# A fused attention and expert-routing kernel: an earlier third sum in phase 0, phase 1 in a fixed list, expert 1 in halves of rows

## The chip, the core and the metric

The kernel runs on one core of a Trainium2 chip. A core has TensorE (PE in the rows, with PEld for its weight loads), VectorE (DVE), ScalarE (ACT), GpSimd (POOL) and SyncE (SP, which here only issues DMAs). Each engine takes its instructions in the order of its own list and waits on semaphores for the others. The metric is the device time of one execution in microseconds, lower is better.

## The reference

Attention over a band of 128 positions gives x (4608 tokens by 512). Then a greedy routing: all 4608 x 8 pairs of token and expert are walked in falling order of their logit; a token goes to the expert of the first pair at which it is still free and the expert has under 576 tokens. Each expert is a two-layer network with a ReLU.

```python
logits = x @ w_gate
order = np.argsort(-logits.flatten())
for idx in order:
    tok, e = (int(idx) // E, int(idx) % E)
    if assigned[tok] >= 0 or counts[e] >= cap:
        continue
    assigned[tok] = e
    counts[e] += 1
...
for e in range(E):
    mask = assigned == e
    h = np.maximum(x[mask] @ w1[e], 0.0)
    out[mask] = h @ w2[e]
```

## The kernel before

Attention takes the first 185 us or so; the change leaves it as it is. Behind it the work is a chain of eight *phases* of routing and eight experts. A phase finds which expert fills up next and at which logit: it counts on PE, by products of 0/1 matrices with ones, how many tokens lie above each of 64 thresholds, narrows the interval, and does that three times (`few`, with the 16 best candidates of each partition). Then it sums the members (`totals`), numbers them (`members`, `positions`, `hits`) and writes the row numbers of the 576 tokens of that expert to `idx` (`rows`). `later` masks the logits for the next phase; two additions of it run on POOL from phase 1 on. Phase 0 (`phase0`) is written apart: it does part of its sums during attention, and guesses the first expert after one search step, so that the first two tiles of rows ("early tiles") and the expert's weights are asked for before the search ends.

An expert takes five tiles of rows. POOL gathers each tile from DRAM into `g`; PE transposes it into a PSUM tile (`pg`, one buffer, or `po`); ACT casts it to `xh`, and DVE takes the rest `xl` from the same PSUM tile (`flip` and `under`; `turn` does both, tile by tile). Weights come in four chunks a layer through `raw` (four buffers) and are split as well: ACT casts the high part (`high`), DVE makes the low part in two halves (`low`; rows `hl<-raw,hl`). Each product is then three matmuls (high by high, high by low, low by high). Layer 1 runs over f = 0 to 7; in `layer1` both column groups of rows (0 to 287, 288 to 575) go through in turn for each f. Layer 2 runs over the five tiles and POOL scatters each finished tile. `keep_warm(n)` puts n matmuls of zeros on PE.

What sets the order: instructions given through `OrderedCore` stand on PE, DVE and ACT in the order in which the program writes them; through `OrderedTensor` only PE's do; given through plain `nc` a scheduler places them by its own estimates. In `first_expert` all is in written order, and generators are stepped by hand: `go` steps phase 0, `next(route)` steps phases 1 to 7, which run one behind the other in the generator `route`. A step issues everything up to the next `yield`. After `first_expert` the kernel before goes over to `OrderedTensor`: in expert 0's layer 2, 40 steps, the tables at L426 to L429 say at which step a piece of `route` is written (`ROUTE_2`), a chunk asked for (`LOAD_2`), split (`SPLIT_2`), the gather issued (`GATHER_2`) and a tile transposed (`TURN_2`). From expert 1 on `slot` does this by due times (`W_LOAD`, `W_SPLIT`) and by the waits that `route` yields.

## Time and profile before

| what | value |
|---|---|
| three runs | 707.56 to 711.46 us, median 709.33 |
| profiled execution | 710.49 us |
| its span (first to last instruction) | 708.6 us |
| PE busy, share of the span | 94% |
| DVE, ACT, POOL busy | 65%, 46%, 21% |

The share of busy time is a mean over stages, and a matmul at the lower clock is counted as busy like one at the higher. So the rows below read stages and single waits. A row of a timeline begins with the start in us and the time in us, then engine, line, operation, output and inputs by the names above; x4 at its end means four instructions merged, and the square bracket holds how long the engine stood idle before it and for whom. Most lines of this stretch carry L461, the line of the helper that keeps the written order, so the names tell them apart. A row of a table by stage has the stretch and its length, then busy us and (instructions) of PE, PEld, DVE, ACT and POOL, the mean granted clock of PE as a share of 2.4 GHz, and the DMA engines' busy share and GB/s.

### The profile page before, as it was taken

How to read it: one execution, taken by the hardware profiler on the slowest of the kernel's cores; microseconds unless marked ns; L12 is line 12 of the kernel's file. 1: busy time of each engine (PE TensorE's matmuls, PEld its weight loads, DVE VectorE, ACT ScalarE, POOL GpSimd, SP SyncE). 2: the span in 40 equal slices, each digit the busy share in tenths (PEclk: the TensorE clock that was granted, in tenths of full speed). 3: DMA queues.
4: the chain of work that ended last, by engine and by line, in shares of the span. 5: the costliest groups of instructions: out<-in, count | busy, mean ns of one | idle time of the engine just before them, and what ended most of it. 6: DMA issues, size and time to landing. Idle time of an engine off the chain costs nothing.

```text
span 708.6 us, 18904 instructions
## 1 busy us (share of the span) xinstructions
PE 667.4 (94%) x7272; PEld 584.4 (82%) x7273; DVE 460.2 (65%) x1903; ACT 326.3 (46%) x992; POOL 150.3 (21%) x337
## 2 busy tenths in 40 slices
PE   8999999999947998599899999999999999999996
PEld 5899889988845976388679879988988988988986
DVE  6778888888876877575778859756864724523210
ACT  6998898988832521422423324314324324323211
POOL 4122222222201102301411324032033023011011
PEclk9999999999975999699999999999999999999999
DMA  8475757575324403700913617145134434401001
GB/s 292 161 229 175 225 178 224 176 229 177 116 78 137 145 8 103 255 9 7 313 46 127 200 57 244 58 134 175 64 119 130 125 98 136 140 21 40 8 24 48
DMA packets 35139, 92.72 MB, mean 131 GB/s; under 512 B 3808, under 2 KB 13152, under 8 KB 35040
## 3 DMA queue, kind: packets, MB, share of 16 engines
q1 hardware_dynamic: 29152, 72.55, 31.7%
q0 software_dynamic: 5888, 18.88, 8.0%
q8 instruction: 59, 0.97, 0.6%
q14 instruction: 40, 0.33, 0.1%
HBM read 72.54 MB, written 18.87 MB: 129 GB/s over the span
## 4 chain that ended last, share of the span: by engine, by line
PE 79%; DVE 9%; issue 4%; DMA 4%; ACT 3%; SPq 0%; POOL 0%; POOLq 0%; DVEq 0%; ACTq 0%
PE ph L1105 22%; PE po L1147 8%; PE po L1148 8%; PE pt L53 6%; PE x L53 6%; PE po L1150 6%; PE s L53 6%; PE pt L160 6%; PE ph L461 4%; PE po L461 2%; DMA g<-x,idx 2%; ACT u L147 2%; PE pg L1077 2%; DVE hl L1042 1%; DMA raw<-in_w_dram 1%
## 5 line engine op out<-in xcount | busy, mean ns | idle before, releaser
L1105 PE MATMUL ph<-xh,hl 128*128 128x288 f32 x896 | 164.3, 298 | 0.0
L1105 PEld LDWEIGHTS ph<-xh,hl 128*128 128x128 f32 x896 | 134.0, 189 | 0.9
L147 ACT ACTIVATE u<-u,mn 128x192 f32<-128x192 f32 (+2 forms) x288 | 124.1, 440 | 5.8 <-DVE mn L137 5.8
L1147 PE MATMUL po<-hl,hh 128*128 128x512 f32 (+1 forms) x288 | 115.2, 400 | 0.5 <-ACT hh L1111 0.5
L1148 PE MATMUL po<-hl,hh 128*128 128x512 f32 (+1 forms) x288 | 111.4, 387 | 0.0
L1111 ACT ACTIVATE hh<-ph 128x288 fp32r<-128x288 f32 x112 | 40.4, 409 | 132.3 <-PE ph L1105 132.2
L1105 PE MATMUL ph<-xl,hl 128*128 128x288 f32 x448 | 97.8, 297 | 0.0
L137 DVE CUSTOM_DVE_ANT_0 u<-s,bm 128x192 f32<-128x192 f32 (+1 forms) x248 | 71.8, 345 | 30.5 <-PE s L53 29.9
L1150 PE MATMUL po<-hl,hlo 128*128 128x512 f32 (+1 forms) x232 | 89.3, 385 | 0.0
L1159 POOL DMA_INDIRECT out_dram<-o,idx x38 | 41.3, 1086 | 204.4 <-ACT o L1154 131.5
L1042 DVE TENSOR_TENSOR hl<-raw,hl 128x512 fp32r<-128x512 f32 x112 | 73.6, 683 | 13.5 <-ACT hl L1036 13.0
L1105 PEld LDWEIGHTS ph<-xl,hl 128*128 128x128 f32 x448 | 72.4, 189 | 0.0
L1084 DVE TENSOR_TENSOR xl<-pg,xh 128x512 fp32r<-128x512 f32 (+1 forms) x35 | 22.3, 636 | 74.3 <-ACT xh L1078 74.0
L1122 DVE SCALAR_TENSOR_TENSOR hlo<-ph,hh 128x288 fp32r<-128x288 f32 x112 | 43.1, 416 | 39.6 <-ACT hh L1111 39.2
L1036 ACT CAST hl<-raw 128x1024 fp32r<-128x1024 f32 x56 | 57.4, 1049 | 20.4 <-DMA raw<-in_w_dram 16.1
L1154 ACT COPY o<-po 128x512 f32<-128x512 f32 (+1 forms) x33 | 18.9, 574 | 103.2 <-PE po L1150 51.6
L1147 PEld LDWEIGHTS po<-hl,hh 128*128 128x128 f32 x288 | 54.5, 189 | 10.5 <-ACT hh L1111 0.7
L1148 PEld LDWEIGHTS po<-hl,hh 128*128 128x128 f32 x288 | 54.6, 189 | 9.4
L53 PE MATMUL s<-qk 64*64 64x192 f32 (+1 forms) x992 | 60.0, 326 | 0.6 <-DVE mn L137 0.5
L147 ACT ACTIVATION_READ_ACCUMULATOR u<-u,mn 128x1 f32 x288 | 56.4, 196 | 0.0
L1058 POOL DMA_INDIRECT g<-x,idx x38 | 40.4, 1062 | 72.1 <-PE pg L1077 22.9
L160 PE MATMUL pt<-ident_sb,u 128*128 128x128 f32 x368 | 52.8, 279 | 0.7 <-ACT u L147 0.4
(308 smaller groups left out, 1120.0 us busy)
## 6 DMA issues: line engine op xcount, KB each, us to landing
raw<-in_w_dram SPq DMA_DIRECT2D x64, 512.0 KB, 4.2
qk<-in_qk_dram SPq DMA_DIRECT2D x32, 576.0 KB, 5.1
v<-in_v_dram SPq DMA_DIRECT2D x32, 288.0 KB, 4.0
x<-xb SPq DMA_DIRECT2D x14, 512.0 KB, 3.6
x<-xb SPq DMA_DIRECT2D x8, 128.0 KB, 3.4
x<-xb SPq DMA_DIRECT2D x4, 256.0 KB, 2.3
g<-x,idx POOLq DMA_INDIRECT x38, 5.1
out_dram<-o,idx POOLq DMA_INDIRECT x38, 2.9
```

The source lines that it names most:

```text
L53: put(nc.tensor.matmul(out, w, a, start=start, stop=stop, skip_group_check=True))
L137: put(nc.vector.tensor_tensor_reduce(out=weights(n, t, h), in0=x[:, c:c + 64 * m].rearrange("q (j k) -> q j k", k=64), in1=bm[n % NP][:, y ...
L147: put(nc.scalar.activation(u, u, AF.Exp, bias=st["mn"][:, i:i + 1], scale=-1.0, accum_out=st["sm"][:, i:i + 1]))
L160: put(nc.tensor.transpose(ps[:, c:c + 128], u[:, o + 128 * j:o + 128 * j + 128], ident))
L461: return lambda *a, **k: self.tc.keep_in_program_order(getattr(self.engine, name)(*a, **k))
L1036: self.nc.scalar.copy(hl[:, 0, :], raw)
L1042: self.nc.vector.tensor_tensor(hl[:, 1, c:c + 512], raw[:, c:c + 512], hl[:, 0, c:c + 512].bitcast(F32), ALU.subtract)
L1105: self.nc.tensor.matmul(pp[t], w[:, a, j, fo:fo + 128], x[:, j, cut[t]:cut[t + 1]], start=(j == 0 and a == 0 and x is xh), stop=(j == 3 an ...
L1122: self.nc.vector.scalar_tensor_tensor(d, pp[t][:, c0:c1], 0.0, o[:, c0:c1].bitcast(F32), ALU.max, ALU.subtract)
L1147: nc.tensor.matmul(out, a, wh, start=(f == 0), stop=False)
L1148: nc.tensor.matmul(out, a, wl, start=False, stop=(f == 7 and t == 4))
L1150: nc.tensor.matmul(out, hl[:, f, 128 * t:128 * t + 128], wh, start=False, stop=(f == 7))
```

## The change

Four things change. In phase 0 `yield` is added behind the sum of each search step, and the calls in `first_expert` are regrouped so that the last step's sum is written ahead of the second early tile's transposes; the zero matmuls are shared out anew, and one operation (`hi`) goes behind `members`. Expert 0's second weights are asked for one piece earlier, and all their low halves are written ahead of phase 1's third piece. `OrderedTensor` goes: expert 0's layer 2 stays in written order on PE, DVE and ACT; only the pieces of `route` behind phase 1's row numbers, and the gathers, are left to the scheduler. Phase 1 is stepped at 26 steps at the latest instead of 29, the gather follows at once, and two pieces of phase 2 (`ROUTE_3`) and the weights of expert 1 come behind. In expert 1 phase 2 is stepped in every slot (`SOONER`), and its layer 1 runs over the first half of the rows for all f, then over the second.

```diff
-ZEROS = 1, 4, 1, 3, 4
...
-ROUTE_2 = 11, 13, 15, 17, 19, 21, 22, 25, 29
...
+ZEROS = 2, 4, 1, 2, 5
...
+ROUTE_2 = 11, 12, 14, 15, 17, 18, 19, 22, 26
+ROUTE_3, SOONER = (33, 37), (1, 2)
...
@@ -804,6 +806,7 @@
                 next(n)
             except StopIteration as e:
                 n = e.value
+            yield
             if s == 1:
                 lo2 = self.small("lo")
                 nc.vector.scalar_tensor_tensor(lo2, w, n[:, 0:1], low, ALU.mult, ALU.add)
@@ -812,8 +815,8 @@
         sel, rest = (rt.tile([128, NT], BF, name=name, bufs=1) for name in ("sel0", "rsel"))
         nc.vector.tensor_scalar(sel, key[:, :, 0], 1.0, n[:, 0:1], ALU.add, ALU.is_ge)
         nc.vector.tensor_tensor(rest, self.rest, sel, ALU.mult)
+        m, ex = self.members(am, v[:, 0:1], rest, NT)
         nc.vector.scalar_tensor_tensor(self.hi, w, n[:, 0:1], low, ALU.mult, ALU.add)
-        m, ex = self.members(am, v[:, 0:1], rest, NT)
         sp = self.bank()
         self.positions(sp, m, ex, NT)
         nc.tensor.matmul(sp[:, 64:65], self.C["ones"], self.run[:, NT - 1:NT], start=True, stop=True)
@@ -894,6 +897,8 @@
         self.rows(ip, hits, NT, 5, idx)
         self.idx[k] = [idx[:, t:t + 1] for t in range(5)]
         self.later(k, L, T1, Dc, keyv, mx)
+        if k == 1:
+            yield 0
 
     def later(self, k, L, T1, Dc, keyv, mx):
 
@@ -1121,14 +1126,17 @@
                     c0, c1 = c0 - cut[t], c1 - cut[t]
                     self.nc.vector.scalar_tensor_tensor(d, pp[t][:, c0:c1], 0.0, o[:, c0:c1].bitcast(F32), ALU.max, ALU.subtract)
 
-    def layer1(self, w1):
+    def layer1(self, w1, halves=False):
 
         self.hidden()
         cut = 0, 288, 576
-        for f in range(8):
-            yield from self.steps1(w1, f, cut, (0, 1))
-            self.rest1(self.pp, f, cut, (0, 1))
+        for f, ts in [(f, (t,)) for t in range(2) for f in range(8)] if halves else [(f, (0, 1)) for f in range(8)]:
+            for _ in self.steps1(w1, f, cut, ts):
+                if not halves:
+                    yield
+            self.rest1(self.pp, f, cut, ts)
             yield
+
 
     def layer2(self, w2, h, idx, last=False, fine=False):
         nc = self.nc
@@ -1207,11 +1215,6 @@
         o += w
 
 
-class OrderedTensor:
-    def __init__(self, tc):
-        self.vector, self.scalar, self.sync, self.tensor = tc.nc.vector, tc.nc.scalar, tc.nc.sync, Ordered(tc, tc.nc.tensor)
-
-
 def first_expert(tc, P, C, r, m, route):
 
     nc = tc.nc
@@ -1250,16 +1253,16 @@
     m.idle = P["ps_h"].tile([128, 512], F32, name="ph")
     W = [m.high(raw[c]) for c in range(2)]
     go(2)
+    m.low(W[0], raw[0], 0)
     m.keep_warm(ZEROS[0])
-    m.low(W[0], raw[0], 0)
-    go()
+    go(2)
+    m.low(W[0], raw[0], 1)
     m.keep_warm(ZEROS[1])
-    m.low(W[0], raw[0], 1)
     go(2)
     m.low(W[1], raw[1], 0)
     a0 = m.flip(*ga[0], "o")
     m.keep_warm(ZEROS[2])
-    go()
+    go(2)
     a1 = m.flip(*ga[1])
     m.keep_warm(ZEROS[3])
     go()
@@ -1295,14 +1298,14 @@
     rest(4, 0)
     b = m.flip(*gb[0], "o")
     m.under(*b)
+    late = marked(1)
+    second += ask(late, 1, range(1, 4))
     layer(6, 0)
     rest(5, 0)
     b = [m.flip(*gb[1], "o"), m.flip(*gb[2])]
     m.under(*b[0])
     rest(6, 0)
     m.under(*b[1])
-    late = marked(1)
-    second += ask(late, 1, range(1, 4))
     layer(7, 0)
     rest(7, 0)
     V, lows = [], []
@@ -1310,16 +1313,17 @@
         layer(f, 1)
         if f == 0:
             go()
-        if f % 2 == 0:
-            V.append(m.high(second[f // 2]))
-            lows += [(V[-1], second[f // 2], half) for half in range(2)]
+        if f in HIGHS_2:
+            V.append(m.high(second[len(V)]))
+            lows += [(V[-1], second[len(V) - 1], half) for half in range(2)]
         if f:
             rest(f - 1, 1)
-        for _ in range(CHOICE_1.get(f, 0)):
+        if f in CHOICE_1:
             next(route)
-        for _ in range(LOWS_2.get(f, 0)):
+        for _ in range(LOWS_2[f]):
             m.low(*lows.pop(0))
     rest(7, 1)
+    next(route)
     return V
 
 
@@ -1344,6 +1348,8 @@
         st["wait"] -= 1
         if st["wait"] <= 0 and (k + 1 not in r.idx or k + 2 not in r.idx and i >= AHEAD[min(k, 2)]):
             st["wait"] = next(route, 0)
+            if k == 1 and k + 1 not in r.idx:
+                st["wait"] = SOONER[i == 0]
         for e, layer, c, due in W_LOAD:
             e += k
             if i >= due and e in r.ei and len(raws.get((e, layer), ())) == c:
@@ -1373,28 +1379,30 @@
             next(route)
     else:
         V = first_expert(tc, P, C, r, m, route)
-        r.nc = m.nc = OrderedTensor(tc)
     i = 0
     for _ in m.layer2(V, m.h, r.idx[0], fine=True):
         i += 1
         if i in ROUTE_2 and not exact:
             next(route)
-        if i == GATHER_2:
+        if i == ROUTE_2[-1]:
+            r.nc = nc
             gathers[0] = m.turn(m.gather(r.idx[1]))
+        if i in ROUTE_3:
+            next(route)
         for _ in range(LOAD_2.get(i, 0)):
             load(1, 0)
         if i in SPLIT_2:
             part(1, 0)
         if i in TURN_2:
             next(gathers[0])
+    r.nc = m.nc = nc
     while len(W[1, 0]) < 4:
         part(1, 0)
     for _ in gathers[0]:
         pass
-    r.nc = m.nc = nc
     for k in range(1, E):
         i = 0
-        for _ in m.layer1(W.pop((k, 0))):
+        for _ in m.layer1(W.pop((k, 0)), k == 1):
             slot(k, i)
             i += 1
         for _ in range(9):
```

The order on PE behind the counts of phase 0's last search step (sat is their verdict, whose sum with the ones is meant; po and pg are the two early tiles, zero the zero matmuls, ex the input of the positions). Before:

```order
L461 MATMUL po<-ident_sb,g 128x128 x4
L461 LDWEIGHTS zero
L461 MATMUL ph<-zero 128x512
L461 MATMUL pg<-ident_sb,g 128x128 x4
L461 LDWEIGHTS zero
L461 MATMUL ph<-zero 128x512
L461 LDWEIGHTS zero
L461 MATMUL ph<-zero 128x512
L461 LDWEIGHTS zero
L461 MATMUL ph<-zero 128x512
L461 LDWEIGHTS c_ones
L461 MATMUL m<-sat,c_ones 128x1
```

and now:

```order
L463 MATMUL po<-ident_sb,g 128x128 x4
L463 LDWEIGHTS zero
L463 MATMUL ph<-zero 128x512
L463 LDWEIGHTS c_ones
L463 MATMUL m<-sat,c_ones 128x1
L463 MATMUL pg<-ident_sb,g 128x128 x4
L463 LDWEIGHTS zero
L463 MATMUL ph<-zero 128x512
L463 LDWEIGHTS zero
L463 MATMUL ph<-zero 128x512
L463 LDWEIGHTS c_ones
L463 MATMUL m<-ex,c_ones 128x36
```

The sum of sat has moved ahead of the second tile and of three zero matmuls; two of the zeros now stand between the tile and ex.

The order on DVE at the end of phase 1 (loOH and mv are the inputs of the row numbers, io to idx their end; am and OH belong to phase 2's first piece, as do the b, ne, cand and ext that stand further up before; hl are weight halves of expert 1, xl its tiles). Before:

```order
L736 TENSOR_TENSOR loOH<-c_i_429,slo 128x2304
L728 TENSOR_TENSOR mv<-hOH,c_cc 128x36x10
L730 TENSOR_SCALAR mv<-hOH,craw 128x36x10
L515 TENSOR_TENSOR OH<-c_eb,am 128x288
L1042 TENSOR_TENSOR hl<-raw,hl 128x512
L749 COPY io<-m 64x20
L1042 TENSOR_TENSOR hl<-raw,hl 128x512
L751 TENSOR_TENSOR ia<-m,io 64x20
L1042 TENSOR_TENSOR hl<-raw,hl 128x512
L754 SCALAR_TENSOR_TENSOR idx<-ia 64x5 x2
L1042 TENSOR_TENSOR hl<-raw,hl 128x512 x5
L1084 TENSOR_TENSOR xl<-pg,xh 128x4x128
```

and now, from the masks that follow idx:

```order
L463 TENSOR_TENSOR flag<-flag,ov 128x1
L463 TENSOR_TENSOR hl<-raw,hl 128x512 x2
L510 TENSOR_REDUCE b<-L_72 128x36
L512 TENSOR_TENSOR ne<-L_72,b 128x288
L524 TENSOR_REDUCE ext<-b 128x1
L514 SCALAR_TENSOR_TENSOR cand<-ne,c_eb 128x288
L516 TENSOR_REDUCE am<-cand 128x36
L517 TENSOR_TENSOR OH<-c_eb,am 128x288
L463 TENSOR_TENSOR hl<-raw,hl 128x512 x2
L1047 TENSOR_TENSOR hl<-raw,hl 128x512
L463 TENSOR_TENSOR xl<-pg,xh 128x4x128
```

Before idx now stand phase 1's own operations alone; phase 2's first piece and the weight halves have moved behind it, all ahead of the first tile's xl.

The order on POOL from the scatter of expert 0's first tiles on (g are gathers of expert 1's tiles, Lt and L the masks of `later`, out_dram scatters). Before:

```order
L1159 DMA out_dram<-o,idxa 4608x512 x2
L914 TENSOR_SCALAR Lt<-T_5503 128x288
L909 TENSOR_TENSOR L_5612<-L_72,pen 128x288
L915 TENSOR_TENSOR L_72<-Lt,L_5612 128x288
L1159 DMA out_dram<-o,idx 4608x512
L1058 DMA g<-x,idx 128x512 x4
L1058 DMA g<-x,idx 64x512
```

and now:

```order
L1167 DMA out_dram<-o,idxa 4608x512 x2
L919 TENSOR_SCALAR Lt<-T_5495 128x288
L1167 DMA out_dram<-o,idx 4608x512
L1063 DMA g<-x,idx 128x512
L914 TENSOR_TENSOR L_5604<-L_72,pen 128x288
L1063 DMA g<-x,idx 128x512
L920 TENSOR_TENSOR L_72<-Lt,L_5604 128x288
L1063 DMA g<-x,idx 128x512 x2
L1063 DMA g<-x,idx 64x512
```

The two additions that make L now stand between the gathers instead of ahead of them.

## Rows read from the trace of the kernel before

**Rows 1.** Table by stage: expert 0's second layer, expert 1, expert 6.
```profile
255.60:307.20 51.60, 38.90 (x198) 28.48 (x197) 34.67 (x110) 13.69 (x19) 12.62 (x13) 0.87 0.36 128
307.20:369.10 61.90, 57.72 (x381) 49.56 (x379) 42.65 (x168) 18.07 (x31) 12.10 (x12) 0.97 0.31 105
598.10:651.60 53.50, 53.50 (x327) 48.40 (x326) 21.63 (x48) 17.53 (x33) 5.01 (x5) 1.00 0.24 82
```

**Rows 2.** Timeline of PE at the end of phase 0's search.
```profile
220.64 1.06 PE L461 MATMUL pg<-ident_sb,g 128*128 128x128 f32 x4
...
222.91 0.18 PE L461 MATMUL m<-sat,c_ones 64*128 64x1 bf16 x1
224.41 0.19 PE L461 MATMUL m<-ex,c_ones 128*128 128x36 bf16 x1 [1.33 <-DVE ex L461]
...
224.50 1.87 PE L461 MATMUL ph<-zero 128*128 128x512 bf16 x4
```

**Rows 3.** Timeline of DVE in the same stretch.
```profile
219.91 0.15 DVE L461 TENSOR_SCALAR sat<-mx 64x1 bf16<-64x1 f32 x1
223.13 0.25 DVE L461 TENSOR_SCALAR sel<-kq,m 128x36 bf16<-128x36 bf16 x1 [3.07 <-PE m L461]
```

**Rows 4.** Timeline of PE in expert 0's second layer.
```profile
259.91 0.50 PE L461 MATMUL po<-hl,hh 128*128 128x512 f32 x1 [1.17 <-DVE hl L461]
...
264.88 0.42 PE L461 MATMUL m<-OHf,ind 128*128 128x16 bf16 x8
...
266.69 0.17 PE L461 MATMUL m<-sat,c_ones 64*128 64x1 bf16 x1
...
268.53 0.42 PE L461 MATMUL m<-OHf,ind 128*128 128x16 bf16 x8
...
276.06 0.62 PE L461 MATMUL po<-hl,hh 128*128 128x512 f32 x2
...
276.75 0.62 PE L461 MATMUL po<-hl,hh 128*128 128x512 f32 x2
...
278.80 0.19 PE L461 MATMUL m<-ex,c_ones 128*128 128x36 bf16 x1 [1.19 <-DVE ex L702]
...
282.79 0.61 PE L461 MATMUL m<-mv,loOH 128*128 128x40 bf16 x18 [0.91 <-DVE mv L730]
...
294.36 1.11 PE L461 MATMUL pg<-ident_sb,g 128*128 128x128 f32 x4 [6.98 <-DMA g<-x,idx]
```

**Rows 5.** Timeline of DVE, phase 1's first piece to expert 1's third tile.
```profile
244.37 0.68 DVE L461 TENSOR_REDUCE b<-L 128x36 f32<-128x288 f32 x1
...
247.00 0.18 DVE L461 TENSOR_REDUCE ext<-b 128x1 f32<-128x36 f32 x1
...
278.04 0.62 DVE L508 TENSOR_REDUCE b<-L 128x36 f32<-128x288 f32 x1
...
284.75 0.17 DVE L751 TENSOR_TENSOR ia<-m,io 64x20 f32<-64x20 f32 x1
...
287.02 0.33 DVE L754 SCALAR_TENSOR_TENSOR idx<-ia 64x5 int32<-64x5 f32 x2
287.38 3.10 DVE L1042 TENSOR_TENSOR hl<-raw,hl 128x512 fp32r<-128x512 f32 x5
...
301.60 0.69 DVE L1084 TENSOR_TENSOR xl<-pg,xh 128x512 fp32r<-128x512 f32 x1
```

**Rows 6.** Timeline of POOL: the last mask addition, first and last of five gathers.
```profile
277.13 0.84 POOL L915 TENSOR_TENSOR L<-Lt,L 128x288 f32<-128x288 f32 x1
...
288.13 1.42 POOL L1058 DMA_INDIRECT g<-x,idx  x1 [8.94 <-issue]
...
294.12 0.91 POOL L1058 DMA_INDIRECT g<-x,idx  x1 [0.30 <-issue]
```

**Rows 7.** Timeline of PE in expert 1's second layer.
```profile
351.54 1.11 PE L1077 MATMUL pg<-ident_sb,g 128*128 128x128 f32 x4 [3.53 <-DMA g<-x,idx]
```

**Rows 8.** Table by stage, the stretch around that wait.
```profile
350.00:355.00 5.00, 3.46 (x11) 2.93 (x12) 2.37 (x7) 0.59 (x1) 2.46 (x3) 0.66 0.97 363
```

More of the change, by code (lines that the diff above doesn't have):

```diff
@@ L422 @@
 AHEAD = 18, 0, 0
-ZEROS = 1, 4, 1, 3, 4
-CHOICE_1 = {1: 1, 4: 1, 6: 1}
-LOWS_2 = {3: 2, 5: 2, 6: 2, 7: 2}
-ROUTE_2 = 11, 13, 15, 17, 19, 21, 22, 25, 29
-GATHER_2, TURN_2 = 30, (36, 37, 38, 40)
-LOAD_2 = {24: 2, 30: 1, 34: 1}
-SPLIT_2 = 33, 35, 37, 39
+ZEROS = 2, 4, 1, 2, 5
+CHOICE_1 = 1, 4
+HIGHS_2 = 0, 3, 4, 5
+LOWS_2 = 0, 0, 0, 2, 1, 2, 2, 1
+ROUTE_2 = 11, 12, 14, 15, 17, 18, 19, 22, 26
+ROUTE_3, SOONER = (33, 37), (1, 2)
+LOAD_2 = {20: 2, 33: 1, 37: 1}
+SPLIT_2 = 31, 33
+TURN_2 = 36, 38, 40
 W_LOAD = [(0, 1, 0, 0), (0, 1, 1, 2), (0, 1, 2, 6), (0, 1, 3, 10),
```

## The prediction

> **What bounds the kernel now.** I read the table by stage first. TensorE (PE) is the bound everywhere, so a stage loses time only where PE waits or runs at the lower of its two clock levels (1.2 instead of 2.4 GHz). From the start of expert 0's second layer to where expert 1's first layer runs freely (255.6 to 307.2) PE is busy 38.90 of 51.60 us at a mean granted clock of 0.87. Expert 1 (307.2 to 369.1) takes 61.90 us; expert 6, with next to no routing beside it, takes 53.50 at clock 1.00 [rows 1]. These two stages and the head of phase 0 are what the change touches.
>
> Phase 0, by the timelines of PE and VectorE (DVE): the last search step's indicator, sat, is ready on DVE at 220.06, but its sum goes out on PE only at 222.91, behind the transposes of the second early tile and three zero matmuls. DVE waits 3.07 us for it (sel, 223.13), and then PE waits 1.33 us for ex [rows 2, 3].
>
> Expert 0's second layer, by PE's timeline: PE waits 1.17 us for a weight half at 259.91. Phase 1's pieces stand between its steps: the first count at 264.88, waits of 1.19 and 0.91 us before the positions (278.80) and the row numbers (282.79), and at last 6.98 us without work before the first gathered tile at 294.36 [rows 4]. DVE's timeline says why the gather is late. Phase 2's first operation, b at 278.04, stands between phase 1's own. ia is done at 284.92, but a weight half that waits for its cast is next in DVE's list (the order of before shows it), and the row numbers idx are done only at 287.35 [rows 5]. POOL (GpSimd) then writes five gathers from 288.13 to 295.03, one per 1.5 us, the first tile arriving 6.2 us after its start [rows 4, 6].
>
> Expert 1, by PE's timeline and a short window: the same once more with phase 2, a wait of 3.53 us before 351.54, and a granted clock of 0.66 in 350 to 355 [rows 7, 8].
>
> **The change part by part.** All times are those of the profiled execution (710.49 us, span 708.6); the runs' median is 709.33, so 1.2 come off at the end.
>
> *Phase 0.* On PE one tile's transposes and one zero matmul now stand between the last count and sat's sum, instead of two tiles' and four zeros. They keep PE until about 220.6, so the sum goes out 2.3 us earlier. The chain from sel to the positions (223.13 to 224.41, 1.3) would end near 222.0, but the second tile's transposes and two zeros come first on PE, until about 222.6: the positions go out 1.8 earlier. Then five zeros follow in place of four (1.87 for four, 0.47 each) [rows 2], which leaves 1.4 for the first layer. The clock is at its lower level there; if it rises earlier with the denser stream, up to 0.9 more comes, if later, as much goes. Taken: 1.5 (0.5 to 2.4). hi behind ex, and the request for the second layer's weights one layer piece earlier, cost nothing: DVE and SP have idle time there that covers them, and without it 0.2 would be lost.
>
> *Weight halves ahead of phase 1's third piece.* All eight halves of expert 0's second weights now stand on DVE ahead of phase 1's ev. The wait of 1.17 goes: 1.2. What is late next is phase 1's first indicator, behind the last rest on DVE, some 1.2 later in that list than now; but PE asks for it only after 11 steps of 0.69 (276.06 to 276.75) [rows 4], by my count a microsecond after it is ready.
>
> *Phase 1 in fewer steps.* The first count comes at 264.88 - 1.5 - 1.2 = 262.2. From it to the row numbers are 15 steps in place of 18: 10.4, and 1.2 for phase 1's own matmuls. With fewer steps between them PE must now wait for DVE. From sat's sum to the next count take 266.69 to 268.53 = 1.84, with two steps under it: 0.4 of wait, twice; 0.1 at each of four single steps, 0.3 at T, 0.1 where 1.19 was (phase 2 no longer cuts in), 0.4 where 0.91 was. Together 2.0. Row numbers on PE at 262.2 + 10.4 + 1.2 + 2.0 = 275.8; they take 0.6, DVE 0.8 after them: idx at 277.2 in place of 287.35 [rows 4, 5].
>
> *What follows in the fixed lists.* The scatter of output tile 2 stands ahead of the gathers on POOL and is done by then. POOL then has gather, add, gather, add, three gathers; the adds make phase 2's L. At 1.5 for a gather and 0.84 for an add [rows 6] phase 2's b can start at 277.5 + 1.5 + 0.8 + 1.5 + 0.8 = 282.1. That is the new wait: DVE's list has b and its five companions, then three weight halves, then xl of the first tile, so these stand still meanwhile, and PE's further transposes with them. The six took 244.37 to 247.18 = 2.8 in phase 1, three halves are 1.9 (3.10 for five), xl 0.69 [rows 5]: xl of the first tile ends at 287.5. Each further tile costs what it costs now: three took 294.36 to 302.29, 2.6 each, since the transposes share one buffer and xl must empty it. xl of the third ends at 292.7, where it is 302.29 now [rows 4, 5]: 9.6 earlier. Rows in halves need only these three tiles to begin, and four output matmuls that now come later (0.9) are then done: 10.5 at the start of expert 1, the 1.5 and 1.2 included. Bounds: if DVE's list is clear when the first tile lands (277.5 + 6.2, transposes 1.1, cast and xl 1.3: 286.1), each tile takes 2.0, and phase 0 gives its most: 14. If ScalarE's casts of the next weights, which stand between the casts of the tiles and wait for loads, hold two tiles up by 1.3 each and phase 0 gives its least: 7.
>
> A gather written while DVE made weight halves took 1.42, one with DVE idle 0.91 [rows 5, 6]. The Trainium skill (SBUF — State Buffer, Who interferes with whom) says that a DVE instruction with two SBUF inputs holds up only GpSimd work that reads SBUF, and infers that descriptor writing is not such work. This trace does not bear it out: the halves have two SBUF inputs. By the rule the two gathers ahead of b would be 0.5 shorter each and the sum 1.0 larger.
>
> *Halves for expert 1.* Matmuls and weight loads keep number and size, only the loops are turned round. The last weight chunk is wanted after some 10 us of the layer instead of 19; its halves stand on DVE ahead of the third tile's xl. Nothing.
>
> *Phase 2 behind phase 1.* It starts in expert 0's second layer and then goes on in every slot, so its rows come at the end of expert 1's first layer, not in its second. The loss there now is 3.5 of wait and about 1.5 from 3 us at the lower clock: 5.0 [rows 7, 8]. In PE's new list 27 output matmuls (6.2) and 12 of the first layer (1.6) stand between row numbers and the first transposes, against some 2.3 until the gather starts and 6.2 to land: a wait near 0.7. The denser steps cost some 1.3 more, by the waits of phase 1 above. Taken: 3.0 (0 to 5.0). Phase 3 also runs sooner; its work is only moved.
>
> Sum: 10.5 + 3.0 = 13.5, so 697.0 as profiled and 695.8 as a median.
>
> **Rivals.** *Tiles as they land* (0.20): POOL's adds are early enough and DVE is no bound; 14 + 5 = 19, 690.3. For it: with DVE idle a gather takes 0.91, which brings b near 281. Against: DVE's list after b is what it is.
> *Given back* (0.17): the front gains 7 and expert 1 waits for its gather as before; 702.3. For it: casts and loads in one line on ScalarE, 6.2 us to land beside a full weight load. Against: phase 2 is half an expert earlier.
> *The list does nothing* (0.04): PE's steps, not DVE's list, set idx; only 1.5 and 1.2 remain, 706.6. Against: from ia to idx alone 2.1 us pass by order only [rows 5].
> *Slower* (0.04): b's wait for POOL's adds. Each microsecond by which they come after 282 moves b, the three halves and all xl, and PE behind them; from 296 on the 13.5 are gone, at 300 the time is 714. For it: POOL waited 0.8 after idx before it began [rows 5, 6]. Against: I find nothing else that POOL could be waiting for at 277.
>
> **How the numbers follow.** The forecast has 0.55, with its own range 692 to 699. The range 687 to 703 takes in the second and third case and leaves out the last two and the tails. About 0.5% (3.5 us) can be told from no change. Faster: 0.55 + 0.20 + 0.17 = 0.92; the fourth case is within 0.5%: same 0.04; slower 0.04.
>
> **What would show it.** sat's sum one zero after the counts. idx near 277, with no operation of phase 2 ahead of it on DVE. b waiting for POOL's add near 282, xl of the first tile near 287, of the third near 293. In expert 1's second layer no wait above 1.5 us for a gather, and clock 1.00. I am wrong if idx comes after 282, or if expert 1's first layer starts after 298 on PE.

## The result and the profile after

The changed kernel takes 698.4 us in the median of four runs (697.95 to 699.89) against 708.44 for the kernel before on the same chip: ratio 0.9855, 95% interval 0.982 to 0.9889. Timed once more beside other kernels it took 697.14 against 708.73: 0.9838 (0.9801 to 0.9875). Forecast were 695.8 and 687 to 703. The profiled execution took 698.43, its span 696.7.

Table by stage of the changed kernel (columns as in [rows 1]): expert 0's second layer up to where expert 1's first layer runs freely, the rest of expert 1, expert 6.

```profile
252.30:296.00 43.70, 38.67 (x201) 29.17 (x200) 32.15 (x115) 12.80 (x17) 13.43 (x13) 0.88 0.45 151
296.00:356.70 60.70, 57.85 (x389) 48.84 (x390) 49.40 (x209) 19.61 (x34) 13.73 (x15) 1.00 0.33 112
584.40:637.90 53.50, 53.50 (x325) 48.41 (x324) 21.62 (x48) 17.69 (x33) 5.01 (x5) 1.00 0.25 82
```

The two stages lasted 113.5 and now last 104.4; expert 6 is the same 53.5. PE stands idle for 5.0 + 2.9 in place of 12.7 + 4.2 [rows 1]. The other gain lies ahead of them. PE at the end of phase 0's search, to be read against [rows 2]:

```profile
220.50 0.18 PE L463 MATMUL m<-sat,c_ones 64*128 64x1 bf16 x1
...
221.53 1.06 PE L463 MATMUL ph<-zero 128*128 128x512 bf16 x2
222.38 0.24 PE L463 MATMUL m<-ex,c_ones 128*128 128x36 bf16 x1
...
222.51 1.53 PE L463 MATMUL ph<-zero 128*128 128x512 bf16 x5
...
226.76 0.61 PE L463 MATMUL m<-mv,loOH 128*128 128x24 bf16 x18
```

sat's sum goes out at 220.50 instead of 222.91, the positions at 222.38 instead of 224.41, with no idle time ahead of them. In the kernel before, phase 0's last row numbers went out at 229.99, and the first layer began at the lower level, with the granted clock at 0.50 up to 228.3 (a window of it and those row numbers):

```profile
227.00:228.00 1.00, 1.00 (x7) 1.00 (x6) 1.00 (x2) 0.07 (x1) 0.00 (x0) 0.50 0.56 127
```
```profile
229.99 0.61 PE L461 MATMUL m<-mv,loOH 128*128 128x24 bf16 x18
```

Now, in short windows, it comes back at 223.1, while the five zeros run:

```profile
222.00:223.00 1.00, 1.00 (x7) 0.45 (x6) 1.00 (x3) 0.36 (x1) 0.00 (x0) 0.50 0.00 0
223.00:224.00 1.00, 1.00 (x6) 0.55 (x5) 0.90 (x6) 0.00 (x0) 0.00 (x0) 0.93 0.00 0
```

The row numbers come at 226.76, and the second layer starts at 252.29 instead of 255.61: 3.3 sooner.

PE in expert 0's second layer, as [rows 4]: first count, row numbers, transposes of the first two tiles, first matmul of expert 1.

```profile
259.90 0.42 PE L463 MATMUL m<-OHf,ind 128*128 128x16 bf16 x8
...
273.57 0.62 PE L463 MATMUL m<-mv,loOH 128*128 128x40 bf16 x18 [0.21 <-DVE loOH L463]
...
280.57 0.66 PE L463 MATMUL pg<-ident_sb,g 128*128 128x128 f32 x4 [0.36 <-DMA g<-x,idx]
...
285.46 1.11 PE L463 MATMUL pg<-ident_sb,g 128*128 128x128 f32 x4 [3.01 <-DVE xl L463]
...
291.07 1.33 PE L1110 MATMUL ph<-xh,hl 128*128 128x288 f32 x4 [1.23 <-ACT xh L463]
```

That last matmul in the kernel before:

```profile
302.45 0.44 PE L1105 MATMUL ph<-xh,hl 128*128 128x288 f32 x1
```

DVE, as [rows 5]: the row numbers, two weight halves, phase 2's b, two more weight halves, and xl of the first three tiles.

```profile
274.83 0.33 DVE L463 SCALAR_TENSOR_TENSOR idx<-ia 64x5 int32<-64x5 f32 x2
...
276.27 2.32 DVE L463 TENSOR_TENSOR hl<-raw,hl 128x512 fp32r<-128x512 f32 x2
280.31 0.68 DVE L510 TENSOR_REDUCE b<-L 128x36 f32<-128x288 f32 x1 [1.71 <-POOL L L920]
...
282.92 1.28 DVE L463 TENSOR_TENSOR hl<-raw,hl 128x512 fp32r<-128x512 f32 x2
...
284.73 0.68 DVE L463 TENSOR_TENSOR xl<-pg,xh 128x512 fp32r<-128x512 f32 x1
...
287.23 0.69 DVE L463 TENSOR_TENSOR xl<-pg,xh 128x512 fp32r<-128x512 f32 x1 [0.31 <-ACT xh L463]
...
291.05 0.69 DVE L463 TENSOR_TENSOR xl<-pg,xh 128x512 fp32r<-128x512 f32 x1 [0.73 <-ACT xh L463]
```

POOL, as [rows 6]:

```profile
275.94 1.00 POOL L1063 DMA_INDIRECT g<-x,idx  x1 [1.50 <-issue]
276.93 1.11 POOL L914 TENSOR_TENSOR L<-L,pen 128x288 f32<-128x288 f32 x1
278.19 1.25 POOL L1063 DMA_INDIRECT g<-x,idx  x1 [0.15 <-issue]
279.46 0.82 POOL L920 TENSOR_TENSOR L<-Lt,L 128x288 f32<-128x288 f32 x1
...
283.10 1.30 POOL L1063 DMA_INDIRECT g<-x,idx  x1 [0.30 <-issue]
```

idx is done at 275.16 instead of 287.35, with nothing of phase 2 ahead of it. PE's wait for the gather, 6.98 before, is 0.36. New waits follow: b waits 1.71 for POOL's add, PE waits 3.01 for the first tile's xl, and xl of the third waits for its cast on ACT. ACT's timeline says what that cast waited for:

```profile
284.78 1.05 ACT L1041 CAST hl<-raw 128x1024 fp32r<-128x1024 f32 x1 [1.98 <-DMA raw<-in_w_dram]
...
289.49 1.04 ACT L1041 CAST hl<-raw 128x1024 fp32r<-128x1024 f32 x1 [2.29 <-DMA raw<-in_w_dram]
290.44 0.58 ACT L463 CAST xh<-pg 128x512 fp32r<-128x512 f32 x1
```

The casts at 284.78 and 289.49 (L1041) are of expert 1's *second* weights; each waits about 2 us for its load, and the tile's cast (xh) stands behind the second. They are not wanted before 321. Expert 2's gather is no longer waited for in expert 1 [rows 7], and the clock is 1.00 there from 296 on [rows 8].

### The profile page after: what moved, and what is told of

It is laid out like the page before. It is cut to its first block, busy times and chain, and to the rows that moved or that the text cites. A ratio compares the mean times of both kernels' runs of the same rounds, so it can differ in the third digit from the quotient of the medians.

```text
span 696.7 us, 18902 instructions
## 1 busy us (share of the span) xinstructions
PE 664.7 (95%) x7274; PEld 582.6 (84%) x7274; DVE 459.6 (66%) x1903; ACT 326.7 (47%) x992; POOL 150.5 (22%) x337
## 3 DMA queue, kind: packets, MB, share of 16 engines
q1 hardware_dynamic: 29152, 72.55, 32.4%
## 4 chain that ended last, share of the span: by engine, by line
PE 79%; DVE 11%; ACT 3%; DMA 3%; issue 2%; POOL 1%; SPq 0%; POOLq 0%; ACTq 0%; DVEq 0%
PE ph L1110 21%; PE po L1155 8%; PE po L1156 8%; PE po L1158 6%; PE pt L53 6%; PE x L53 6%; PE s L53 6%; PE pt L160 6%; PE ph L463 4%; DVE hl L1047 2%; PE po L463 2%; DMA raw<-in_w_dram 2%; ACT u L147 2%; PE pg L1082 2%; DVE hlo L1127 1%
## 5 line engine op out<-in xcount | busy, mean ns | idle before, releaser
L1110 PE MATMUL ph<-xh,hl 128*128 128x288 f32 x896 | 168.0, 300 | 1.2 <-ACT xh L463 1.2
L1110 PEld LDWEIGHTS ph<-xh,hl 128*128 128x128 f32 x896 | 136.2, 190 | 2.5 <-ACT xh L463 1.6
L1110 PE MATMUL ph<-xl,hl 128*128 128x288 f32 x448 | 102.2, 298 | 0.0
L137 DVE CUSTOM_DVE_ANT_0 u<-s,bm 128x192 f32<-128x192 f32 (+1 forms) x248 | 71.8, 345 | 29.9 <-PE s L53 29.4
L1047 DVE TENSOR_TENSOR hl<-raw,hl 128x512 fp32r<-128x512 f32 x108 | 71.9, 681 | 11.8 <-ACT hl L1041 11.4
L1110 PEld LDWEIGHTS ph<-xl,hl 128*128 128x128 f32 x448 | 74.2, 189 | 0.0
L1089 DVE TENSOR_TENSOR xl<-pg,xh 128x512 fp32r<-128x512 f32 (+1 forms) x32 | 20.2, 632 | 76.7 <-ACT xh L1083 73.3
L1127 DVE SCALAR_TENSOR_TENSOR hlo<-ph,hh 128x288 fp32r<-128x288 f32 (+1 forms) x112 | 43.8, 417 | 38.7 <-ACT hh L1116 37.3
L1041 ACT CAST hl<-raw 128x1024 fp32r<-128x1024 f32 x54 | 55.3, 1050 | 16.5 <-DMA raw<-in_w_dram 12.7
L1162 ACT COPY o<-po 128x512 f32<-128x512 f32 (+1 forms) x29 | 16.6, 572 | 83.6 <-PE po L1158 53.3
```

Of the source, the lines that this page charges most:

```text
L137: put(nc.vector.tensor_tensor_reduce(out=weights(n, t, h), in0=x[:, c:c + 64 * m].rearrange("q (j k) -> q j k", k=64), in1=bm[n % NP][:, y ...
L1041: self.nc.scalar.copy(hl[:, 0, :], raw)
L1047: self.nc.vector.tensor_tensor(hl[:, 1, c:c + 512], raw[:, c:c + 512], hl[:, 0, c:c + 512].bitcast(F32), ALU.subtract)
L1110: self.nc.tensor.matmul(pp[t], w[:, a, j, fo:fo + 128], x[:, j, cut[t]:cut[t + 1]], start=(j == 0 and a == 0 and x is xh), stop=(j == 3 an ...
L1127: self.nc.vector.scalar_tensor_tensor(d, pp[t][:, c0:c1], 0.0, o[:, c0:c1].bitcast(F32), ALU.max, ALU.subtract)
```

## The experiments

A profile's absolute times differ by up to 3 us from one profile to the next before the change is reached, so the stages are compared from the start of expert 0's second layer. Times of expert 1's and 2's first matmul and of the last ones are us behind that start, from the profiled execution.

| kernel | median us | ratio to before (95%) | expert 1 | expert 2 | last |
|---|---|---|---|---|---|
| before | 708.4 to 710.0 | 1 | 46.8 | 113.4 | 447.0 |
| changed | 698.4 | 0.9855 (0.9820 to 0.9889) | 38.8 | 104.4 | 436.8 |
| c1 changed again | 697.1 | 0.9838 (0.9801 to 0.9875) | 38.3 | 103.4 | 435.9 |
| e1 phase 0 only | 706.8 | 0.9958 (0.9938 to 0.9978) | 45.7 | 112.7 | 446.3 |
| e2 phase 2 not sooner | 704.9 | 0.9926 (0.9900 to 0.9951) | 37.3 | 104.2 | 442.8 |
| e3 no halves | 697.1 | 0.9828 (0.9805 to 0.9851) | 37.7 | 102.8 | 435.1 |
| e7 two zeros less | 698.0 | 0.9826 (0.9800 to 0.9851) | 37.8 | 101.6 | 433.6 |
| e4 casts behind | 696.1 | 0.9811 (0.9779 to 0.9843) | 37.6 | 100.4 | 432.8 |
| e5 adds on DVE | 697.3 | 0.9826 (0.9794 to 0.9858) | 38.0 | 103.6 | 436.1 |
| e6 phase 2 behind | 697.3 | 0.9828 (0.9798 to 0.9858) | 35.5 | 101.0 | 434.4 |
| e8 = e4 + e5 | 692.9 | 0.9772 (0.9738 to 0.9806) | 33.9 | 99.9 | 432.2 |
| e9 = e4 + e6 | 699.7 | 0.9865 (0.9825 to 0.9905) | 35.0 | 104.6 | 437.1 |
| e10 | 696.9 | 0.9826 (0.9792 to 0.9860) | 35.4 | 103.8 | 436.0 |
| e11 steps of before | 698.5 | 0.9854 (0.9832 to 0.9876) | 38.3 | 103.0 | 435.2 |

**e1, phase 0 alone.** The kernel before with this, with hi behind ex, and with the two halves of the first weight chunk (`m.low`) each moved one line up:

```diff
-ZEROS = 1, 4, 1, 3, 4
+ZEROS = 2, 4, 1, 2, 5
...
                 n = e.value
+            yield
...
-    go()
+    go(2)
+    m.low(W[0], raw[0], 1)
     m.keep_warm(ZEROS[1])
-    m.low(W[0], raw[0], 1)
...
-    go()
+    go(2)
     a1 = m.flip(*ga[1])
```

> The kernel before with the changed order of phase 0 alone (third sum ahead of the second early tile's transposes, zeros 2, 4, 1, 2, 5, hi behind ex). The changed kernel begins expert 0's second layer 3.2 us sooner than before, more than the 1.5 (0.5 to 2.4) forecast. Theory: all of it comes from here, 2.0 from the earlier positions and 1.2 from PE running without a hole into the first layer, so that the granted clock is back at 1.00 at 223 instead of 228; nothing behind takes it back: layer 2 starts near 252.4, the last matmul ends 3.2 sooner, the time is near 705.2. Rival: expert 0's second weights, asked for only a piece sooner, are then late: the wait for a weight half before 260 grows from 1.2 to about 3, the last matmul ends at most 1.5 sooner, 707.

3.2 us between the medians, ratio 0.9958: the theory's size. In the profile 2.8 of it are there at the last matmul, counted from phase 0's first row numbers. In this profile the positions come 11.0 behind the first row numbers of phase 0 (12.7 before), its last row numbers 16.3 (18.3 before, 15.2 in the changed kernel).

**e7, two zeros less.** The changed kernel with this edit (all runs that follow are edits of the changed kernel too).

```diff
-ZEROS = 2, 4, 1, 2, 5
+ZEROS = 2, 4, 1, 0, 5
```

> The changed kernel with two zero matmuls (1.06 us on PE) left out between the second early tile and the positions. ex is ready on VectorE near 222.0, so a hole of about 0.5 opens on PE before the positions, which come 0.4 sooner (222.0 instead of 222.38). Theory: the hole, not the order by itself, sets when the clock is back: as before, the first layer then begins at 0.50, and it loses 0.5 to 1.5; row numbers of phase 0 on PE near 227.5 instead of 226.76, the time about 1 slower than the changed kernel. Rival: a short hole changes nothing of the clock: row numbers at 226.4, 0.4 faster.

PE at the positions, and the windows behind them:

```profile
222.49 0.19 PE L463 MATMUL m<-ex,c_ones 128*128 128x36 bf16 x1 [0.41 <-DVE hi L463]
...
227.57 0.61 PE L463 MATMUL m<-mv,loOH 128*128 128x24 bf16 x18
```
```profile
224.00:225.00 1.00, 1.00 (x6) 0.68 (x4) 0.93 (x5) 0.33 (x1) 0.00 (x0) 0.63 0.00 0
```

The hole of 0.41 is there, the clock comes back later than in the changed kernel, and 227.57 is what the theory had. But in e2, e3 and e6, without a hole and with the changed kernel's zeros, the clock comes back 12.8 to 13.3 behind the first row numbers, in e7 13.0, in the changed kernel 11.6. In the 12 other profiles with the new order the last row numbers stand 15.1 to 16.3 behind the first; e7's 15.9 lies among them. So the runs don't support the theory; by itself the profile of e7 would have seemed to.

**e2, phase 2 not sooner.** The changed kernel without the two edits that step phase 2 sooner.

```diff
-ROUTE_3, SOONER = (33, 37), (1, 2)
+ROUTE_3, SOONER = (), (1, 2)
...
-            if k == 1 and k + 1 not in r.idx:
-                st["wait"] = SOONER[i == 0]
```

> The changed kernel with phase 2 not begun in expert 0's second layer and stepped in expert 1 by its own waits as before. Theory: the start of expert 1 stays at 291 on PE (the first operations of phase 2 stand at the same place of VectorE's list), and the wait for expert 2's gather comes back in expert 1's second layer, with the lower clock behind it: 3.0 slower than the changed kernel (0 to 5.0), near 701.4. Rival: the sooner steps cost by their own waits (1.13 before 318.99, 1.35 near 336) as much as the gather's wait did: no difference, 698.4.

5.0 to 6.2 slower than the changed kernel by the ratios (0.9926 against 0.9855 and 0.9838), more than forecast. The gather's wait is back on PE:

```profile
344.42 1.11 PE L1082 MATMUL pg<-ident_sb,g 128*128 128x128 f32 x4 [4.67 <-DMA g<-x,idx]
```

Expert 1 loses by it, and experts 2 and 3 then take 61.0 and 61.3 instead of 59.0 and 57.1, since the later phases are late too: phase 3's row numbers come 131.4 behind the start instead of 110.3. That part was in no theory.

**e3, no halves.** Expert 1's first layer runs as in the kernel before.

```diff
-        for _ in m.layer1(W.pop((k, 0)), k == 1):
+        for _ in m.layer1(W.pop((k, 0))):
```

> The changed kernel with expert 1's first layer not in halves of rows. Forecast's price: nothing for the loops turned round by themselves; but the forecast's start counted three tiles only. Theory: without halves each step needs all five tiles, whose last xl is done at 296.9, so PE has little to do from 292 to 297 and loses 2 to 4: 700.4 to 702.4, with the lower clock lasting past 296. Rival: what is lost at the start comes back, since the halves made VectorE's list of hlo and weight halves denser (PE waits 1.13 before 318.99): within 0.5 of the changed kernel.

The first matmul comes at 37.7 (38.8 and 38.3 with halves), the median is 697.1: the rival. The halves of rows neither gain nor cost anything that this measurement can tell.

**c1, the changed kernel again.**

> The changed kernel once more, beside the next three on one chip. The e7 run has the same code from expert 0's second layer on and came 3.2 us sooner from there to the end than the profiled changed kernel. Theory: that is spread of one execution to the next, by how long the granted clock stays at 0.50 after PE stood idle before the first gathered tiles (3 us there, 10 us in the changed kernel): a profile of the same code falls anywhere between 433.5 and 437 us from the start of expert 0's second layer to the last matmul, and the median stays at 698.4 within 1.5. Rival: the two zeros fewer did it: this run shows 436.8 and 10 us at 0.50 again.

The median differs by 1.3. The profile shows the rival's sign in the clock: 10.2 us at the lower level, as long as in the first one, with the last matmul at 435.9. But e3 speaks against the rival: it has the zeros of the changed kernel and its instructions up to expert 1's first matmul, at 290.8, and its lower level ends before that, at 289.9, after 3.4 us. So executions of the same instructions differ in how long the lower level lasts, though the two profiles of the changed kernel happen to agree. What sets it stays open. A difference of 1 to 3 us behind the gather between two single profiles can therefore be this and not the edit.

**e4, casts behind the tiles.** `m.last` is the last tile's cast on ACT, kept by flip.

```diff
     def part(e, layer):
+        if (e, layer) == (1, 1):
+            with tc.issue_after(m.last.ins):
+                W[e, layer].append(m.split(raws[e, layer][len(W[e, layer])]))
+            return
```

> The changed kernel with ScalarE's casts of expert 1's second weights held behind the cast of the last gathered tile. Theory A (the forecast's): VectorE's list and the half clock set the tiles, the casts cost at most the 0.6 that the third tile's cast waited behind one of them; expert 1's first matmul comes 37.1 to 38.2 after the start of expert 0's second layer, where it is 37.7 to 38.8; time within 1 of the changed kernel. Theory B (the forecast's bound): casts that wait for loads hold two tiles by 1.3 each: 35.1 to 36.2, 2.6 faster.

The first matmul at 37.6: theory A. VectorE's list alone still holds the second tile:

```profile
285.75 1.12 PE L463 MATMUL pg<-ident_sb,g 128*128 128x128 f32 x4 [3.01 <-DVE xl L463]
```

PE's wait for phase 3's indicator in expert 1's second layer is 0.51 (1.67 and 0.80 in the two profiles of the changed kernel), expert 1 lasted 62.8 (65.7 and 65.1). The interval of the time overlaps the changed kernel's, so a gain is not shown.

**e5, mask adds on DVE.** The two additions for phase 2's mask leave POOL.

```diff
-            eng = nc.vector if k == 0 else self.tc.nc.gpsimd
+            eng = nc.vector if k < 2 else self.tc.nc.gpsimd
...
-            if k == 0:
+            if k < 2:
                 nc.vector.scalar_tensor_tensor(self.L1, T1, 100.0 * BIG, L2, ALU.mult, ALU.add)
```

> The changed kernel with the two adds (and the product) of phase 2's mask on VectorE for this phase instead of GpSimd. b then waits for nobody, and the gathers on GpSimd stand one behind the other. Theory A (b's wait of 1.71 holds the first tile's xl): counted along VectorE's list from idx, xl of the first tile ends 8.8 after idx instead of 10.3, the weight halves beside GpSimd take 0.65 each instead of 1.16; expert 1's first matmul 1.4 sooner, 36.3 to 37.4 after the start of expert 0's second layer; time about 697. Rival: the tiles are held by casts and by PE at half clock, so 37.7 to 38.8 as now.

DVE and then ACT:

```profile
276.13 0.68 DVE L510 TENSOR_REDUCE b<-L 128x36 f32<-128x288 f32 x1
...
277.83 1.28 DVE L463 TENSOR_TENSOR hl<-raw,hl 128x512 fp32r<-128x512 f32 x2
...
281.78 0.69 DVE L463 TENSOR_TENSOR xl<-pg,xh 128x512 fp32r<-128x512 f32 x1
...
285.75 0.69 DVE L463 TENSOR_TENSOR xl<-pg,xh 128x512 fp32r<-128x512 f32 x1 [1.79 <-ACT xh L463]
```
```profile
284.19 1.04 ACT L1041 CAST hl<-raw 128x1024 fp32r<-128x1024 f32 x1 [1.90 <-DMA raw<-in_w_dram]
285.14 0.58 ACT L463 CAST xh<-pg 128x512 fp32r<-128x512 f32 x1
288.28 1.05 ACT L1041 CAST hl<-raw 128x1024 fp32r<-128x1024 f32 x1 [2.56 <-DMA raw<-in_w_dram]
289.23 0.58 ACT L463 CAST xh<-pg 128x512 fp32r<-128x512 f32 x1
```

b waits for nobody, xl of the first tile comes 2.5 sooner (29.9 behind the layer's start, 32.4 before the edit). Then xl of the second waits 1.79: its cast at 285.14 stood behind a weight cast that waited 1.90 for its load, and the third's behind one that waited 2.56. All of the 2.5 is gone: the first matmul comes at 38.0, as the rival said.

**e6, phase 2 behind the third tile.** `m.last` is here the latest xl, kept by under; the old two lines on ROUTE_3 are gone.

```diff
-ROUTE_3, SOONER = (33, 37), (1, 2)
+ROUTE_3, SOONER = (40, 41), (1, 2)
...
             next(gathers[0])
+        if i in ROUTE_3:
+            with tc.issue_after(m.last.ins):
+                next(route)
```

> The changed kernel with phase 2's first operations (b and its companions) held behind xl of the third gathered tile on VectorE, instead of ahead of the first. Theory A: weight halves and xl then wait for no GpSimd add; xl of the first tile ends when the tile has landed, 2.9 sooner (near 30.2 after the start of expert 0's second layer instead of 33.1), expert 1's first matmul 34.8 to 35.9, PE's idle stretch shorter by as much; phase 2's row numbers come some 6 later than now, still before expert 2's tiles are wanted: 695.5. Rival: phase 2 is late again, expert 2's gather is waited for by 2 or more in expert 1's second layer and the phases behind stay late as in the run with phase 2 not sooner: 698.4 or more.

The first matmul at 35.5, as theory A counted: 1.8 below the earliest of the runs above, and by an edit of VectorE's list alone. The casts of the second and third tile stood behind weight casts here too, but these waited 0.87 and 1.37 for their loads, not 1.90 and 2.56 as in e5: this hold has no fixed length. Expert 2 then lasts 60.0 instead of 59.0, and the time, 697.3, shows no gain.

**e8.** The edits of e4 and e5 together.

> Both edits at once on the changed kernel: ScalarE's casts of expert 1's second weights held behind the cast of the last gathered tile, and the adds of phase 2's mask on VectorE. Each alone left expert 1's first matmul where it was (37.6 and 38.0 after the start of expert 0's second layer); with the adds on VectorE the first tile's xl came 2.5 sooner, and then the casts of the second and third tile stood behind weight casts that waited 1.9 and 2.6 for their loads. Theory: two holds in a row, each of which covers the other; with both gone the tiles follow at 2.2 each: xl of the third ends 35 after the start, the first matmul at 35.0, 2.7 sooner than either alone; from there to the end as with the casts behind (expert 1 62.8): last matmul near 430, time near 693.5. Rival: GpSimd's gathers or PE at half clock are a third hold at the same place: first matmul at 37 or later, time 696.

```profile
283.04 0.66 PE L463 MATMUL pg<-ident_sb,g 128*128 128x128 f32 x4 [0.55 <-DVE xl L463]
...
285.15 0.66 PE L463 MATMUL pg<-ident_sb,g 128*128 128x128 f32 x4 [0.22 <-DVE xl L463]
286.48 0.80 PE L1110 MATMUL ph<-xh,hl 128*128 128x288 f32 x4 [0.67 <-ACT xh L463]
```

33.9: 3.7 and 4.1 sooner than with either edit alone, where neither by itself had moved it beyond the spread (37.3 to 38.8). So these two edits work only together: with one hold gone the other is left, in e4 the wait of 3.01 for xl, in e5 the casts. About 1.0 of the 3.7 goes with the clock: from the second tile's transposes to the first matmul PE took 3.4 here, at 1.00, and 4.4 in e4, most of it at 0.50. Expert 1 gives much of the gain back (66.0; PE waits 1.16 for an indicator at 334.93). By its median of 692.9 it is the fastest kernel here, below the changed one (0.9806 against 0.982 at the intervals' nearest ends in the first timing; they overlap in the second) and not separated from e4.

**e9 and e10.** e9 has the edits of e4 and e6. e10 has those of e4 and e5, and e6's with `ROUTE_3 = (36, 39)`, which puts phase 2 behind the first tile's xl.

> On the changed kernel: ScalarE's casts of expert 1's second weights held behind the last gathered tile's cast, and phase 2's first operations held behind the third tile's xl (its mask adds stay on GpSimd between the gathers). Theory of two holds: with phase 2 behind, the first matmul came at 35.5, and 1.5 of wait for a tile's cast was left before it; with the casts behind as well it comes at 34.0 to 34.5. But phase 2 comes later, and with phase 2 behind expert 2 lasted 60.0 instead of 59.0: last matmul near 431, time near 694. Rival: the second tile lands only then (1.8 of wait for its load in the run with phase 2 behind), so 35.5 stays and the time is 696.

> On the changed kernel: casts behind the last gathered tile's, mask adds on VectorE, and phase 2's first operations behind xl of the first tile. Theory: xl of the first tile then ends when the tile has landed (29 to 30 after the start of expert 0's second layer), gathers stand one behind the other on GpSimd; phase 2's six operations (2.8) now stand between the first and the second tile: first matmul at 34 to 35, phase 2 late by 3 at most: last matmul near 430, time near 693.5, no better than the casts behind with the adds on VectorE by more than 1. Rival: the six operations cost their whole 2.8 there: first matmul at 37.

Both miss: 699.7 and 696.9 where 694 and 693.5 were expected. Expert 1 starts at 35.0 and 35.4, but phase 2's row numbers come 72.1 and 71.8 behind the start, no sooner than the changed kernel's 72.4 and 5 later than e8's 66.8. e9's PE waits for expert 2's gather, and e10's for phase 3's indicator:

```profile
332.40 0.66 PE L1082 MATMUL pg<-ident_sb,g 128*128 128x128 f32 x4 [3.99 <-DMA g<-x,idx]
```
```profile
340.04 0.43 PE L600 MATMUL m<-OHf,ind 128*128 128x16 bf16 x8 [2.10 <-DVE ind L576]
```

**e11, the steps of before.** Phase 1's pieces stand behind the steps of before, in the fixed order of now.

```diff
-ROUTE_2 = 11, 12, 14, 15, 17, 18, 19, 22, 26
+ROUTE_2 = 11, 13, 15, 17, 19, 21, 22, 25, 29
...
-LOAD_2 = {20: 2, 33: 1, 37: 1}
+LOAD_2 = {24: 2, 33: 1, 37: 1}
```

> The changed kernel with phase 1's pieces behind the same steps of expert 0's second layer as before (11, 13, 15, 17, 19, 21, 22, 25, 29 instead of 11, 12, 14, 15, 17, 18, 19, 22, 26; the first loads of expert 1's weights 4 steps later, since the expert's number comes later), VectorE's fixed list kept. From the first count to the row numbers idx it took 22.5 before and takes 15.3 now. Theory of the list: 18 steps of 0.69 and 1.2 of phase 1's own matmuls, with the waits for VectorE gone, are 13.6 to 14.5 up to the row numbers on PE, and idx comes 1.6 behind them since nothing of phase 2 stands between: idx 15.2 to 16.1 after the first count, expert 1's first matmul at most 1 later than the 37.7 to 38.8 of the changed kernel, time within 1 of it. Theory of the steps (the forecast counted 15 steps in place of 18 as a part of its gain): idx 18 to 19 after the first count, first matmul near 41.5, time near 701.

```profile
261.03 0.42 PE L463 MATMUL m<-OHf,ind 128*128 128x16 bf16 x8
...
276.92 0.62 PE L463 MATMUL m<-mv,loOH 128*128 128x40 bf16 x18 [0.20 <-DVE loOH L463]
```
```profile
278.00 0.33 DVE L463 SCALAR_TENSOR_TENSOR idx<-ia 64x5 int32<-64x5 f32 x2
```

idx is done 17.3 behind the first count, between the two theories (15.3 in the changed kernel, 22.5 before): of 7.2 gained there, 2.0 are the fewer steps and 5.2 the fixed list with its order (3.7 against e1's profile, where the list of before took 21.0). Even the 2.0 don't show in the first matmul (38.3) or the time. But this profile has no stretch at the lower clock behind the gather, where the changed kernel's two have 10.2 us, so what the steps are worth there is not settled by it.

## Why the prediction was right, step by step

- **Phase 0: mis-sized.** Taken 1.5, bounds 0.5 to 2.4. Positions 1.9 sooner, as worked out. The step that was too small is "the clock is at its lower level there; if it rises earlier with the denser stream, up to 0.9 more comes": the clock comes back 3 to 5 us sooner, and the stage up to the last row numbers is shorter by 3.1 in the changed kernel's profile and by 2.0 to 3.2 in the 12 of the experiments.
- **Weight halves:** the 1.17 is gone, and the first count stands 7.6 behind the layer's start instead of 9.3 (9.3 in e1, which lacks this part); taken 1.2, measured 1.7.
- **Phase 1 in fewer steps:** from first count to row numbers 13.67, worked out 13.6; idx 1.6 behind them, 1.4 forecast. Of the gain the forecast laid 2.1 (three steps of 0.69) to the fewer steps; by e11 it is 2.0.
- **What follows in the lists:** b waited for POOL's add, as said; from idx to the first tile's xl 10.3, forecast 10.3. Taken for each further tile: 2.6; it was 3.2 in this execution, at half clock. That ACT's weight casts can hold tiles stood only as a bound. It is a second hold at the same place, and e5 and e8 show it; by e6 its length varies.
- **Halves:** nothing, and nothing it is (e3). The sentence that only three tiles are needed with halves was true without them too: in e3 the first matmul, at 290.82, stands ahead of the fourth tile's transposes at 291.55.
- **Phase 2 behind phase 1:** taken 3.0 (0 to 5.0). In expert 1 before, 4.2 went by idle time and 0.03 of 61.9 = 1.9 by the clock [rows 1, 7, 8]; now 2.9 go from 296 on, at clock 1.00, which is 3.2 less. Counted from expert 1's first matmul to the last, with the slow start up to 296 in it, 400.2 have become 398.0: 2.2 less. e2 says something else: without this part the changed kernel would be 5.0 to 6.2 slower, by more than the kernel before lost in expert 1, since experts 2 and 3 lose as well.
- **The sum:** 13.5 forecast. The last matmuls start at 689.10 instead of 702.65: 13.55. That it fits to 0.1 is luck. Phase 0 (3.3 at the second layer's start) and the weight halves gave 1.8 and 0.5 more than taken; the tiles behind idx gave 1.1 less, from expert 1's first matmul on it was 0.8 less, the row numbers 0.3 less.
- **The time:** 10.0 and 11.6 by medians, less than the sum. The step that failed here is "the runs' median is 709.33, so 1.2 come off": with one run more that median was 708.44, 2.05 below the profiled execution. In the other timings it was 708.7 to 710.0, so this is spread. And 1.7 of the 13.55 are lost behind the last scatter, which is issued until 691.03 with the span's end 5.7 later; before, 704.59 and 4.0:

```profile
690.06 0.97 POOL L1167 DMA_INDIRECT out_dram<-o,idx  x1 [4.57 <-ACT o L1162]
```

In the 12 profiles of the experiments that tail is 4.0 to 5.8, in c1, the changed kernel's second profile, 4.2: spread, which the sum took as fixed.
- **The rivals:** *given back* had ACT's casts right and their price wrong: expert 1's first matmul comes 11.4 sooner (10.5 forecast, 7 in that case), and no gather is waited for in expert 1. *Tiles as they land* fell: b came at 280.31, sooner than the 281 it counted on, but it still waited 1.71 for POOL's add, and DVE's list did bind (PE's wait of 3.01). *The list does nothing* fell with idx at 275.16; *slower* didn't come, with b at 280.31.
- **The rule weighed:** the rule of the Trainium skill (SBUF — State Buffer, Who interferes with whom) would have shortened two gathers by 0.5 each. Gather, add, gather, add took 4.34, by my rows 4.68, so the forecast lost little either way. What the Trainium skill infers there, that weight halves don't hold up the writing of descriptors, is not settled here. A gather that ran beside weight halves for its whole length took 1.30 (283.10, beside the halves at 282.92), but the one at 275.94 ran beside them for two thirds of its time and took 1.00. Over all 14 profiles, 312 gathers with no half beside took 0.90 to 1.11, and 44 with halves beside for nearly their whole length 0.94 to 1.97, median 1.28. A gather also reads its row numbers from idx, so it may fall under the rule itself and not under the inference; no run tells these apart. The rule itself, that such halves and GpSimd work that reads SBUF hold each other up, is borne out: two halves beside GpSimd's add, which reads SBUF, took 2.32, and in e5, beside gathers alone, 1.28; the add took 1.11 beside them and 0.67 before, with no half beside.

## What to carry to other kernels

When an engine waits, look for a second hold of about the same length behind the first: an edit that does nothing by itself (e4's start, e5's start) may be half of one that does. A hold that waits for a load need not keep its length (e6). Work moved sooner on an in-order engine is priced by what stands behind it there, and work moved later by every stage that follows (e2, e9). Before a difference of 2 us between two profiles is explained, profile one of them several times: here two agreed by chance, and only a third execution of the same instructions showed the spread.

## What the hardware showed

- The same instructions got the higher clock back at different times. In 11 profiles with the same program up to there it rose 11.3 to 13.5 us behind phase 0's first row numbers (13.0 in e7, 13.7 in e1, 16.7 in the one of the old order). Behind the first gather PE stood idle for 3.0, and the lower level then lasted 10.2 in both profiles of the changed kernel, 3.4 in e3 and in e7. e3 has the changed kernel's instructions until its lower level ends, and e7 lacks only two zero matmuls far ahead. The same window in the changed kernel, its second profile, e3 and e7:

```profile
290.00:294.00 4.00, 2.92 (x12) 2.92 (x13) 2.43 (x7) 2.77 (x5) 0.93 (x1) 0.50 0.52 174
290.00:294.00 4.00, 3.72 (x16) 3.71 (x17) 2.99 (x9) 2.78 (x4) 0.93 (x1) 0.50 0.53 164
290.00:294.00 4.00, 3.00 (x22) 2.38 (x20) 3.91 (x10) 2.56 (x4) 0.93 (x1) 1.00 0.61 198
290.00:294.00 4.00, 3.24 (x25) 2.81 (x24) 3.92 (x10) 2.61 (x5) 0.93 (x1) 1.00 0.58 183
```
